# Transformer block with a conditioned norm: the first hundred microseconds in a new order, key rows filled by ScalarE, modulation mostly on VectorE

## The chip, the cores and the metric

The kernel runs on one core of a Trainium2 chip. A core has five engines with an instruction stream each: TensorE (PE in the profile; its weight loads are shown apart as PEld), VectorE (DVE), ScalarE (ACT), GpSimd (POOL) and SyncE (SP), which here does nothing but issue transfers. Within a stream instructions go in order, and an instruction that waits holds up all behind it. The metric is the device time of one execution in microseconds (us); less is better. Two kernels are compared by the medians of several executions.

## The reference

2048 tokens of width 512 pass through attention and a gated feed-forward part; one row `c` of 512 numbers conditions both.

```python
mod = silu(c) @ w_mod                       # six rows of 512: sa, ca, ga, sb, cb, gb
h = layernorm(x) * (1 + ca) + sa            # the first modulation: shift sa, scale 1 + ca
q, k, v = split(h @ wqkv)                   # 32 heads of 16
p = softmax(mask(q @ k.T * 16 ** -0.5))     # key at most 255 behind the query
x = x + ga * ((p @ v) @ wo)                 # gate row ga
h = layernorm(x) * (1 + cb) + sb            # second modulation
x = x + gb * ((silu(h @ w1) * (h @ w3)) @ w2)
```

## The kernel before

Tokens are cut into 4 blocks of 512 (16 tiles of 128), the width into 4 pieces of 128, called k below. Full precision comes from splitting each operand into a high part, rounded to the fast matmul type, and a low rest: one product is three matmuls (high by high, low by high, high by low).

The program has three stages. The **opening** (to about 99 us) loads `x` and the weights, makes the first modulation, normalises all four blocks, transposes them to `hT`, multiplies them by the value weights, and prepares the first three units of attention. A **unit** is one group of 4 heads in one block. The **attention** stage then runs 32 units, and the **feed-forward** stage the rest. In the opening the work on one block goes like this:

- `stats` (L626, L627): mean and variance of a tile on DVE; `root` (L633): the inverse root of the variance on POOL; `apply` (L636): the tile normalised, on DVE.
- `turn` (L641): four PE transposes bring piece k of the block's four tiles into one PSUM bank.
- `shifted` (L645): ScalarE reads that bank, multiplies by 1 + ca and adds sa (columns of `modc`), and writes `h`; `part` (L650, L652): DVE casts `h` to the high part of `hT` and subtracts it to get the low part.
- `value` (L657): three matmuls for a token tile and a piece k, 48 for a block; `value_out` (L661) stores the result to `vS`.
- `product` (L483): a unit's projection for queries and keys, 12 matmuls, evacuated by ScalarE (L489 to L495), mixed by POOL (L501) and written by SP (L506) into `ring`, where queries and keys stand as rows.
- `scores` (L539) and `top` (L546): PE products and DVE maxima which give each query's bound; these rows go into `ring` too (L571).

The first modulation is made on PE: `mod_rows` (L667) multiplies 128 x 128 pieces of `w_mod` by a single column of silu(c), 32 matmuls with one output column each, and `mod_out` (L671) puts sa and 1 + ca into `modc`, one pair of columns per k. The second modulation is made on DVE by `mod_cols` (L675): a row of weights multiplied by `crep` and summed, one column per instruction. `crep` is silu(c) on all 128 partitions; `c` is loaded 128 times for it (L710). The gates ga and gb are rows of PE products (`gate_row`, L682). The value weights' high part is cast by ScalarE (`wvh`, L723) and the low part made by POOL (`wvl`, L725). Constant rows of `ring` beside the keys are set by POOL (`ring_fill`, L453 to L457, five instructions per block). Before all this five products of zeros (L715) occupy PE.

The order in the opening is set by a list scheduler: every step has a key (a planned time) and an assumed duration, engines take what is ready by key, and `OFF0` holds a correction to each step's key, empty here. The scheduler only fixes the order in which instructions stand in each stream; waits are semaphores. All buffers of the opening, `stage` among them (the loads of weights, which lie in the part of `vS` not yet used), are given out in that order. The attention stage has another order, by fixed times within a unit of 8 steps: there `gate_load` (L981) spreads a gate row for `jobs` on POOL (L986) which multiply weights by it.

Of the kernel before, what the change touches and what calls it, by code (L numbers as in the profile page):

```python
# [18 lines left out]
P = 128  # L19
# [24 lines left out]
OFF0 = ()  # L44
K0 = dict(wv=(7.0, 8.5), wl=1.0, h0=11.0, hb=19.0, tn=3.0, st=8.0, ap=4.0, mj=(22.0, 24.0), mg=(24.0, 40.0), rf=(13.0, 23.0, 40.0, 60.0),
# [43 lines left out]
class Op:  # L89
    __slots__ = ("eng", "fn", "occ", "key", "lat", "mode", "deps", "need", "est", "start", "users",  # L90
                 "bank", "seq", "tag", "kb", "base", "more", "port", "att", "quick",
                 "frees")
# [12 lines left out]
class Clock:  # L105
# [5 lines left out]
    def run(self, s, occ):  # L111
# [6 lines left out]
        self.busy += occ  # L118
        return occ


class Sched:
# [7 lines left out]
    def op(self, eng, fn, occ, key, reads=(), writes=(), lat=None, mode=0, port=None):  # L130
# [6 lines left out]
        o.att, o.quick, o.frees = False, False, None  # L137
# [24 lines left out]
    def deal(self):  # L162
# [20 lines left out]
        while left:  # L183
# [63 lines left out]
            if o.eng == "PE":  # L247
                more = clock.run(s, o.occ) - o.occ
                o.occ += more
                o.lat += more  # L250
# [83 lines left out]
def block_kernel(ctx: ExitStack, tc: tile.TileContext, x, wqk, wv, wo, w13, w2, c, crow, wmod, wmodt, out):  # L334
# [270 lines left out]
    XS = 6  # L605
    begin = []

    def do(t, eng, fn, reads=(), writes=(), occ=0.5, kb=0, port=None):
        begin.append((t, len(begin), eng, fn, list(reads), list(writes), occ, kb, port))
# [19 lines left out]
    def var(b):  # L629
        nc.vector.tensor_scalar_add(rs[:, b, 0], mv[:, 4 * b:4 * b + 4, 1], EPS)  # L630

    def root(b):
        nc.gpsimd.tensor_tensor(out=rs[:, b, 1], in0=rs[:, b, 0], in1=nhalf, op=ALU.pow)  # L633

    def apply(t):
        nc.vector.tensor_scalar(xt[t], xt[t], mv[:, t, 0:1], rs[:, t // 4, 1, t % 4:t % 4 + 1],  # L636
                                op0=ALU.subtract, op1=ALU.mult)
# [9 lines left out]
    def part(b, k, n):  # L647
        lo = slice(b * BT, b * BT + BT)
        if n == 0:
# [5 lines left out]
    def value(t, k, bk):  # L655
        for m, (w, i) in enumerate(((0, wvh), (0, wvl), (1, wvh))):
# [17 lines left out]
    def mod_cols(j, n, i):  # L674
        nc.vector.tensor_tensor_reduce(out=stage[:, i], in0=stage[:, i], in1=crep, scale=1.0, scalar=0.0,  # L675
                                       op0=ALU.mult, op1=ALU.add, accum_out=modc[:, 2 + j, n:n + 1])
        if j and n == KC - 1:
# [20 lines left out]
    for t in range(4):  # L698
        dma(0.1 + 0.1 * t, load_x(t), [("xt", t)], eng="ACT" if t in (1, 3) else "SP")
    do(0.6, "ACT", lambda: nc.scalar.activation(sc, c_sb, AF.Silu), ["c"], ["sc"], 1.4)  # L700
    n0 = 0.7
    for n in range(KC):
        for j in range(2):
            dma(n0, lambda j=j, n=n: nc.sync.dma_start(stage[:, KC + KC * j + n], wmod[j, n].rearrange(
                "p k c -> p (k c)")), [("stg", KC + KC * j + n)])
            n0 += 0.1
        dma(n0, lambda n=n: nc.sync.dma_start(stage[:, n], wv[:, n]), [("stg", n)])
        n0 += 0.1
    dma(n0, lambda: load_wqk(0, 0), ["wqr"])
    dma(n0 + 0.1, lambda: nc.sync.dma_start(crep, crow.to_broadcast([P, D])), ["crep"])  # L710
    for t in range(4, 6):
        dma(n0 + 0.2, load_x(t), [("xt", t)])
    for n in range(5):
        bk = Bank("at")
        do(0.5 + 0.1 * n, "PE", lambda bk=bk: nc.tensor.matmul(ps(bk)[:4], zero[:, 0], zero[:, 0, 0:1].to_broadcast([P, BT]),  # L715
# [1019 lines left out]
```

## Time and profile before

| | |
|---|---|
| median of 3 runs (range) | 959.72 us (957.61 to 960.27) |
| the profiled execution, its own time | 957.99 us |
| its span, first to last instruction | 956.3 us |
| mean granted TensorE clock | 0.990 |
| PE busy | 940.2 us, 98% of the span |
| DVE, ACT, POOL busy | 738.7, 549.4, 521.6 us |
| first projection product (L483) | starts at 20.95 us |
| first score product of the attention stage (L857) | starts at 98.91 us |

PE is called busy for nearly the whole span, so the busy share says little. What tells is which matmuls fill the time, how long one takes at a given place, and when each stage begins. Rows of the time line have start, duration, engine, line, operation, output and inputs, count, and in brackets the idle time before with what ended it.

### The profile page before, as it was taken

To read this page: it belongs to the slowest core of one execution; us is meant where nothing else is said; L and a number is where in the kernel's file an instruction comes from. 1 tells how busy PE (TensorE), PEld (TensorE's weight loads), DVE (VectorE), ACT (ScalarE), POOL (GpSimd) and SP (SyncE) were. 2 spreads that over 40 slices of the span, in tenths; PEclk is the share of its full clock that TensorE was granted. 3 is DMA by queue.
4 is the path that set the end of the run, shared out by engine and by line. 5 is a ranking of instruction groups with operands and counts; after the bars stand their busy time and mean duration, and the time that the engine had idled before them with its cause. 6 is when DMAs were issued, how large, how long until landed. Compare 5 with 4: busy or idle time off the path is not lost.

```text
span 956.3 us, 17149 instructions
## 1 busy us (share of the span) xinstructions
PE 940.2 (98%) x5322; PEld 724.5 (76%) x5322; DVE 738.7 (77%) x2055; ACT 549.4 (57%) x1247; POOL 521.6 (55%) x737
## 2 busy tenths in 40 slices
PE   9999999999999999999999999999999999999998
PEld 6667777777777776775688888888888888888886
DVE  6976789998989898989578775676579866677555
ACT  3333787878787878786769854424455334433230
POOL 8611686878686868685643855445767222221320
PEclk7999999999999999999999999999999999999999
DMA  9611354444454444445993564656685422322002
GB/s 327 199 58 36 103 169 153 146 152 143 147 178 139 151 145 146 137 132 178 254 263 121 180 204 135 196 165 210 216 278 172 167 63 79 99 73 87 23 23 88
DMA packets 81702, 141.90 MB, mean 148 GB/s; under 512 B 10570, under 2 KB 23242, under 8 KB 81612
## 3 DMA queue, kind: packets, MB, share of 16 engines
q1 hardware_dynamic: 81180, 140.29, 45.5%
q8 instruction: 42, 0.69, 0.3%
q10 hardware_dynamic: 432, 0.53, 0.2%
q14 instruction: 48, 0.39, 0.1%
HBM read 85.99 MB, written 34.61 MB: 126 GB/s over the span
## 4 chain that ended last, share of the span: by engine, by line
PE 83%; POOL 5%; DMA 4%; DVE 3%; issue 2%; ACT 2%; SPq 0%; POOLq 0%; ACTq 0%; DVEq 0%
PE st L1505 12%; PE mx L1505 10%; PE pj L483 7%; PE mx L539 7%; PE st L857 7%; PE mx L1599 7%; PE po L818 6%; PE st L1599 5%; PE pj L1505 3%; PE mx L657 3%; PE po L1505 3%; PE po L1599 2%; PE pj L1599 2%; POOL pt L885 2%; POOL qk L501 2%
## 5 line engine op out<-in xcount | busy, mean ns | idle before, releaser
L546 DVE CUSTOM_DVE_ANT_0 junk<-mx,mskq 128x384 bf16<-128x384 f32 (+1 forms) x483 | 242.1, 527 | 30.7 <-PE mx L539 29.2
L539 PE MATMUL mx<-ring 96*128 96x384 f32 (+1 forms) x483 | 145.1, 341 | 3.5 <-DVE st L875 1.7
L857 PE MATMUL st<-ring 100*128 100x384 f32 (+2 forms) x484 | 145.9, 343 | 0.6 <-ACT pt L878 0.4
L885 POOL TENSOR_SCALAR_AFFINE_SELECT pt<-pt 128x256 f32<-128x256 f32 x268 | 108.3, 407 | 58.7 <-ACT pt L878 48.4
L483 PE MATMUL pj<-hT,wq 128*128 128x512 f32 x384 | 134.3, 408 | 0.0
L539 PEld LDWEIGHTS mx<-ring 96*128 96x128 f32 x483 | 88.0, 189 | 34.3 <-DVE mt L546 21.7
L878 ACT ACTIVATE pt<-st 128x256 f32<-128x256 f32 x255 | 91.4, 387 | 37.6 <-DVE st L875 30.3
L857 PEld LDWEIGHTS st<-ring 100*128 100x128 f32 x484 | 90.3, 190 | 18.2 <-issue 6.7
L1549 POOL TENSOR_TENSOR t<-t,t 128x512 f32<-128x512 f32 x28 | 40.9, 1460 | 110.9 <-DVE t L1537 103.9
L818 PE MATMUL po<-pt,vS 128*17 128x256 f32 (+2 forms) x1408 | 96.4, 387 | 2.9 <-ACT os L925 1.1
L501 POOL TENSOR_TENSOR qk<-qkr,qk 128x512 fp32r<-128x512 f32 x64 | 83.4, 1303 | 16.5 <-ACT qkr L489 16.3
L1096 POOL TENSOR_TENSOR w<-w,w 128x512 fp32r<-128x512 f32 (+2 forms) x35 | 51.6, 1485 | 57.4 <-ACT w L1095 57.4
L483 PEld LDWEIGHTS pj<-hT,wq 128*128 128x128 f32 x384 | 72.0, 192 | 7.2 <-DVE hT L652 0.2
L1537 DVE TENSOR_TENSOR t<-st,t 128x512 f32<-128x512 f32 x55 | 37.8, 690 | 49.4 <-PE st L1505 37.7
L875 DVE COPY_PREDICATED st<-later,st 128x128 f32<-128x128 uint8 x255 | 68.7, 291 | 7.0 <-PE st L857 3.7
L818 PEld LDWEIGHTS po<-pt,vS 128*17 128x17 f32 x1408 | 32.5, 96 | 47.8 <-issue 18.8
L1505 PE MATMUL st<-b,w 128*128 128x512 f32 x234 | 58.8, 389 | 0.0
L902 POOL TENSOR_SCALAR_AFFINE_SELECT sm<-sm 128x256 f32<-128x256 f32 x109 | 41.9, 407 | 27.1 <-ACT sm L892 23.2
L869 ACT ACTIVATE pt<-st 128x384 f32<-128x384 f32 (+2 forms) x113 | 47.1, 433 | 13.7 <-DVE st L865 12.6
L1505 PE MATMUL mx<-b,w 128*128 128x512 f32 x204 | 51.4, 390 | 0.0
L1505 PEld LDWEIGHTS st<-b,w 128*128 128x128 f32 x234 | 43.9, 188 | 9.2
L1577 ACT ACTIVATE qkr<-g 128x512 fp32r<-128x512 f32 x13 | 8.2, 632 | 66.4 <-DVE g L1533 66.4
(345 smaller groups left out, 2168.4 us busy)
## 6 DMA issues: line engine op xcount, KB each, us to landing
ring<-qk SPq DMA_DIRECT2D x192, 128.0 KB
o_dr<-os SPq DMA_DIRECT2D x32, 256.0 KB
w<-wsum SPq DMA_DIRECT2D x14, 512.0 KB
w<-w2g SPq DMA_DIRECT2D x14, 512.0 KB
jb<-in_w SPq DMA_DIRECT2D x24, 256.0 KB
wraw<-in_w SPq DMA_DIRECT2D x7, 768.0 KB
w<-wraw SPq DMA_DIRECT2D x14, 384.0 KB
e<-in_w SPq DMA_DIRECT2D x18, 256.0 KB
```

The source lines that it names most:

```text
L483: nc.tensor.matmul(v["ps"], WQ[g][w][:, n // 3], hTp(i, n // 3, b * BT, BT), start=(n == 0), stop=(n == 3 * KC - 1))
L501: nc.gpsimd.tensor_tensor(out=v[n], in0=v["raw"], in1=v[1].bitcast(F32), op=ALU.subtract)
L539: nc.tensor.matmul(v[i][:, :n], queries(NS, a, gq, 1), keys(NS, hh, a, k0, gq + 1 - k0), start=True, stop=True)
L546: nc.vector.tensor_tensor_reduce(out=junk[:, :n], in0=v[i][:, :n], in1=mskq[:, 3 * P - n:], scale=1.0, scalar=-3e38, op0=ALU.add, op1=ALU. ...
L818: nc.tensor.matmul(po[32 * i:32 * i + DH + 1, qb * P:(qb + nq) * P], vS[:, kb, 4 * g + i], pts[i // 2][:, i % 2, c0:c0 + nq], start=first, ...
L857: nc.tensor.matmul(ps[:, :nq], keys(NM, hh, a, kb, 1), queries(NM, a, kb, nq), start=True, stop=not plus)
L875: nc.vector.copy_predicated(ps[:, 0], later, ps[:, 2])
L878: nc.scalar.activation(pt_of(j, a)[:, hh, :2], v[j, a, hh][:, :2], AF.Exp, scale=SCALE)
L885: nc.gpsimd.affine_select(out=pt[:, :, 2 * m], in_=pt[:, :, 0], **w)
L1096: sch.op(eng, lambda: on_eng(eng).tensor_tensor(out=lo(), in0=src(), in1=hi().bitcast(F32), op=ALU.subtract), tt(eng, n), key, kl + kh, kl ...
L1505: nc.tensor.matmul(ps(bk), WT[s, n][w][:, col], BB[t, k][r], start=start and c == 0, stop=stop and c == 5, skip_group_check=True)
L1599: nc.tensor.matmul(ps(bk), tiles[hk + (h,)][:, i * P:(i + 1) * P], w2_of(last, y, f), start=(m == 0), stop=(m == 5))
```

## The change

The opening gets other steps and another order; the attention stage changes in one key. The parts:

- **Key rows on ScalarE.** `ring_fill` is two ScalarE copies per block of 100 x 2 x 512 elements, from a small constant tile `fills`, in place of five POOL memsets.
- **First modulation.** Only k = 0 stays on PE (8 of 32 matmuls). For k = 1, 2, 3 `mod_cols` makes the columns on DVE (six instructions and three that add 1), from weights that are loaded the other way round.
- **The condition.** `c` is loaded once as a row, and one PE product with a column of ones spreads it to 128 partitions in PSUM; ScalarE's silu writes `crep` from there. The load of 128 copies is gone.
- **Block 0 normalised in pieces.** The inverse root is taken for two tiles at a time; `apply` is a scalar_tensor_tensor on DVE, first for the 128 columns of k = 0 and then for the other 384.
- **High parts on ScalarE.** In blocks 0 and 1 the high part of `hT` is written by ScalarE from PSUM, beside `shifted`; DVE's cast is gone there.
- **Value weights.** `wvl` for k = 0 is on DVE. In block 0 `value` is cut in two steps: the two products that need only the high part of `hT`, and the third.
- **Idle products.** Five of 512 columns go around the row product; ten of 128 columns follow `mod_rows`.
- **Transfers.** Tile 3 of `x` is issued by SP and not by ScalarE's queue.
- **Order.** Other keys, durations and a table `OFF0`.
- **Attention.** `gate_load` moves from 8u + 7.65 to 8u + 7.85, behind the rows of `ring` that were behind it.

On ScalarE the work before and after the first two `shifted` stands like this; before:

```order
L700 ACTIVATE sc<-c_sb 128x4 [waits DMAHW0_49]
L723 ACTIVATE wvh<-vS 128x512 [waits DMAHW7_49]
L723 ACTIVATE wvh<-vS 128x512 [waits DMAHW2_49]
L723 ACTIVATE wvh<-vS 128x512 [waits DMAHW5_49]
L645 ACTIVATE h_246<-st,modc 128x512 [waits PE_49]
L723 ACTIVATE wvh<-vS 128x512 [waits DMAHW0_49]
L468 ACTIVATE wq_261<-wqr 128x512 [waits DMAHW1_49]
L645 ACTIVATE h_266<-mx,modc 128x512 [waits DVE_49,PE_49]
```

and ScalarE now (L491 is `ring_fill`, L842 the silu that writes `crep`, L780 `wvh`, L687 `shifted`, L692 the high part):

```order
L748 ACTIVATE sc<-c_sb 128x4 [waits DMAHW0_49]
L491 ACTIVATE ring<-fills 100x2x512 [waits Pool_49]
L842 ACTIVATE crep<-st 128x512 [waits PE_49]
L491 ACTIVATE ring<-fills 100x2x512 [waits Pool_49]
L780 ACTIVATE wvh<-vS 128x512 [waits DMAHW0_49]
L780 ACTIVATE wvh<-vS 128x512 [waits DMAHW3_49]
L491 ACTIVATE ring<-fills 100x2x512 x2
L780 ACTIVATE wvh<-vS 128x512 [waits DMAHW6_49]
L687 ACTIVATE h_254<-st,modc 128x512 [waits PE_49]
L692 ACTIVATE hT<-st,modc 128x512
```

(Rows that only repeat are left out: each of the first three fills shown is followed by a second one or has one more beside a `wvh`, so that two fills stand ahead of L842, two between it and the first `wvh`, one between the first and second `wvh`, and two ahead of the third.) Seven of the eight fills stand ahead of the first `shifted`.

On DVE the stretch from the inverse roots to the first low part of `hT`; before:

```order
L630 TENSOR_SCALAR rs<-mv 128x4 [waits DVE_49]
L636 TENSOR_SCALAR xt_130<-xt_130,mv,rs 128x512 [waits Pool_49]
L671 TENSOR_TENSOR modc<-mx,plus 128x2 [waits PE_49]
L636 TENSOR_SCALAR xt_135<-xt_135,mv,rs 128x512
L636 TENSOR_SCALAR xt_137<-xt_137,mv,rs 128x512
L636 TENSOR_SCALAR xt_145<-xt_145,mv,rs 128x512
L671 TENSOR_TENSOR modc<-st,plus 128x2 [waits PE_49] x2
L650 CAST hT<-h_246 128x512 [waits Activation_49]
L652 TENSOR_TENSOR hT<-h_246,hT 128x512 [waits DVE_49]
```

and DVE now (L674 `apply`, L783 `wvl`, L721 `mod_cols`, L697 the low part):

```order
L783 TENSOR_TENSOR wvl<-vS,wvh 128x512 [waits DMAHW0_49,Activation_49]
L674 SCALAR_TENSOR_TENSOR xt_137<-xt_137,mv,rs 128x128 [waits Pool_49]
L674 SCALAR_TENSOR_TENSOR xt_137<-xt_137,mv,rs 128x384
L717 TENSOR_TENSOR modc<-st,plus 128x2 [waits PE_49]
L721 ISA vS,modc<-vS,crep 128x512 [waits DMAHW1_49]
L674 SCALAR_TENSOR_TENSOR xt_143<-xt_143,mv,rs 128x128
L674 SCALAR_TENSOR_TENSOR xt_143<-xt_143,mv,rs 128x384
L674 SCALAR_TENSOR_TENSOR xt_141<-xt_141,mv,rs 128x384
L721 ISA vS,modc<-vS,crep 128x512 [waits DMAHW7_49]
L721 ISA vS,modc<-vS,crep 128x512 [waits DMAHW2_49,DMAHW0_49]
L721 ISA vS,modc<-vS,crep 128x512 [waits DMAHW2_49]
L697 TENSOR_TENSOR hT<-h_254,hT 128x512 [waits Activation_49]
```

(Left out: behind each L721 row the reading of its sum, and behind the last two of them an addition of 1, L724.) `wvl` and four modulation columns now stand between the pieces of `apply` and the first low part. On PE what stands before the first value products; before it was 32 `mod_rows` with transposes between them and then projections, and now:

```order
L764 MATMUL po<-zero 4x512 x3
L757 MATMUL st<-vS,plus 128x512 [waits DMAHW2_49,Pool_49]
L764 MATMUL po<-zero 4x512
L713 MATMUL st<-sc,vS 128x1 [waits DMAHW6_49,Activation_49]
L713 MATMUL st<-sc,vS 128x1 [waits DMAHW7_49]
L764 MATMUL po<-zero 4x128 x10
L683 MATMUL st<-ident,xt_133 128x128 [waits DMAHW1_49,DVE_49,Pool_49]
L703 MATMUL st<-wvh,hT 128x512 [waits Activation_49]
L703 MATMUL st<-wvl,hT 128x512
L703 MATMUL st<-wvh,hT 128x512 [waits DVE_49]
```

(Each L713 row has three more behind it, and 16 transposes L683 stand in a row.) From the first score product of the attention stage on, PE, DVE, ScalarE and POOL have the same instructions in the same order as before. On SP the gate's load; before:

```order
L506 DMA ring<-qk_1568 16x4x512 x2
L506 DMA ring<-qk_1536 16x4x512 x2
L981 DMA wqr<-g_dr 128x512
L506 DMA ring<-qk_1576 16x4x512 x2
L1000 DMA wsum<-jb_1399 128x512
```

and now:

```order
L541 DMA ring<-qk_1553 16x4x512 x2
L541 DMA ring<-qk_1521 16x4x512 x2
L541 DMA ring<-qk_1561 16x4x512 x2
L1055 DMA wqr<-g_dr 128x512
L1074 DMA wsum<-jb_1384 128x512
```

One pair of rows has passed it, at six places. The diff, without the table of offsets and without the scheduler's bookkeeping:

```diff
-OFF0 = ()
+OFF0 = (0, 0, 0, 0, 0, 0, -58.96, -114.58, 0, 0, 0, -188.94, 0, 0, 0, 0, 0, 0, 0, 0, -95.27, 0, 0, 62.42, 0,
...
-    def ring_fill(b, n):
-        hh = int(n > 1)
-        k = ring.bitcast(F32)[:, 2 - 2 * hh, :, b * BT:(b + 1) * BT]
-        if n in (0, 2):
-            nc.gpsimd.memset(k[:NM] if hh == 0 else k[:NS], 0.0)
-        elif n == 3:
-            nc.gpsimd.memset(k[NS:NM], 1.0)
-        else:
-            nc.gpsimd.memset(k[NS:NS + 2], 1.0 - hh)
+    def ring_fill(b, hh):
+        nc.scalar.activation(ring[:NM, 2 - 2 * hh, :, b * BT:(b + 1) * BT],
+                             fills[:NM, hh:hh + 1, None].to_broadcast([NM, 2, BT]), AF.Copy)
...
-            (nc.scalar if t in (1, 3) else nc.sync).dma_start(xt[t], x[t * P:(t + 1) * P, :])
+            (nc.scalar if t == 1 else nc.sync).dma_start(xt[t], x[t * P:(t + 1) * P, :])
...
-    def apply(t):
-        nc.vector.tensor_scalar(xt[t], xt[t], mv[:, t, 0:1], rs[:, t // 4, 1, t % 4:t % 4 + 1],
-                                op0=ALU.subtract, op1=ALU.mult)
+    def apply(t, c):
+        m, r, z = mv[:, t, 0:1], rs[:, t // 4, 1, t % 4:t % 4 + 1], xt[t][:, slice(c * P, D if c else P)]
+        if t < 4 and (t, c) not in K0["ag"]:
+            nc.vector.scalar_tensor_tensor(out=z, in0=z, scalar=m, in1=r.to_broadcast([P, D - P if c else P]),
+                                           op0=ALU.subtract, op1=ALU.mult)
+            return
...
-    def part(b, k, n):
+    def part(b, k, n, bk=None):
         lo = slice(b * BT, b * BT + BT)
-        if n == 0:
+        if n == 0 and b in CAST:
+            nc.scalar.activation(hT[:, 0, k, lo], ps(bk), AF.Identity, bias=modc[:, 0, k:k + 1],
+                                 scale=modc[:, 1, k:k + 1])
+        elif n == 0:
             nc.vector.tensor_copy(hT[:, 0, k, lo], hs[b, k])
...
+    loads = [(KC + KC * j + n, wmod[j, n].rearrange("p k c -> p (k c)")) for n in range(1) for j in range(2)]
+    loads += [(KC + KC * j + n, wmodt[4 * KC + 2 * n + j - 2]) for n in range(1, KC) for j in range(2)]
...
+    dma(0.05, lambda: nc.scalar.dma_start(stage[:1, 3 * KC - 1], crow), [("stg", 3 * KC - 1)], kb=4, eng="ACT")
+    ck = Bank("at")
+    do(0.62, "PE", lambda: nc.tensor.matmul(ps(ck), plus[:1, 1:2].to_broadcast([1, P]), stage[:1, 3 * KC - 1], start=True,
+                                            stop=True), [("stg", 3 * KC - 1)], [ck], 0.87)
...
-    dma(n0 + 0.1, lambda: nc.sync.dma_start(crep, crow.to_broadcast([P, D])), ["crep"])
...
+            if n < 1:
+                do(6.0 + 1.4 * n + 0.7 * j, "PE", lambda j=j, n=n, bk=bk: mod_rows(j, n, bk), ["sc", ("stg", i)],
+                   [bk], 0.9, use=0.03)
+            else:
+                do(K0["mc"] + 1.3 * n + 0.6 * j, "DVE", lambda j=j, n=n, i=i: mod_cols(j, n, i), ["crep", ("stg", i)],
+                   [("stg", i), ("mod", n)], 0.80 if j else 0.70, port=True)
...
-    do(13.0, "ACT", lambda: nc.scalar.activation(crep, crep, AF.Silu), ["crep"], ["crep"], 0.48)
+    do(K0["cs"], "ACT", lambda: nc.scalar.activation(crep, ps(ck), AF.Silu), [ck], ["crep"], 0.66)
...
-            at(8 * u + 7.65, lambda u=u: gate_load(int(u > 6)))
+            at(8 * u + 7.85, lambda u=u: gate_load(int(u > 6)))
```

More of the change, by code (lines that the diff above doesn't have):

```diff
@@ L247, in deal @@
             if o.eng == "PE":
-                more = clock.run(s, o.occ) - o.occ
+                more = clock.run(s, o.occ, o.use) - o.occ
                 o.occ += more
@@ L653, in part, with value @@
                                     op=ALU.subtract)
-    def value(t, k, bk):
-        for m, (w, i) in enumerate(((0, wvh), (0, wvl), (1, wvh))):
+    def value(t, k, bk, r=range(3)):
+        for m in r:
+            w, i = ((0, wvh), (0, wvl), (1, wvh))[m]
             nc.tensor.matmul(ps(bk), hTp(w, k, t * P, P), i[:, k], start=(k == 0 and m == 0),
@@ L713, in block_kernel @@
[L713 to L722 removed]
+        loads.insert(3 * n + 2, (n, wv[:, n]))
@@ L734, in block_kernel @@
     do(12.5, "DVE", fill_odd, [], ["odd"], 0.5)
[L735 removed]
+    do(11.0, "POOL", lambda: nc.gpsimd.memset(vS[:, :4, :, DH:], 1.0), [], ["ones"], 0.35)
     for b in range(NB):
         h = K0["h0"] + K0["hb"] * b
[L738 to L739 removed]
+        for n in range(2):
+            do(K0["rf"][b] + 1.0 * n, "ACT", lambda b=b, n=n: ring_fill(b, n), ["sc"], [("fill", b)], 1.03)
         for i in range(4):
```

138 lines of the change are left out of this document (81 added, 57 removed), and 35 rows, old and new, of the table OFF0.

## The prediction

> **What bounds the kernel now.** I read the page's chain first, then the stretches of the three stages, then PE's time line in the opening. The chain that ends last is PE's:
>
> ```profile
> PE 83%; POOL 5%; DMA 4%; DVE 3%; issue 2%; ACT 2%; SPq 0%; POOLq 0%; ACTq 0%; DVEq 0%
> ```
>
> So the change counts only where it lets PE start real work earlier, or leaves PE with fewer gaps. The stretches (busy time of each engine with its count, then granted clock, DMA share, GB/s) say where that can be:
>
> ```profile
> 0.00:41.70 41.70, 40.03 (x158) 27.32 (x158) 33.05 (x63) 12.63 (x20) 34.00 (x45) 0.84 0.81 277
> 41.70:98.90 57.20, 56.42 (x262) 42.70 (x262) 38.91 (x118) 20.61 (x34) 10.06 (x9) 1.00 0.18 57
> 98.90:956.30 857.40, 843.71 (x4904) 654.45 (x4902) 666.73 (x1875) 516.13 (x1194) 477.53 (x684) 1.00 0.46 148
> ...
> 10.00:15.00 5.00, 4.70 (x31) 4.64 (x31) 4.00 (x5) 1.26 (x2) 4.86 (x5) 0.75 1.05 394
> 20.00:25.00 5.00, 5.00 (x18) 4.22 (x19) 3.90 (x7) 1.73 (x3) 4.83 (x7) 0.50 1.06 338
> 25.00:30.00 5.00, 5.00 (x21) 4.02 (x20) 4.90 (x13) 0.97 (x2) 2.39 (x3) 0.88 0.78 277
> ```
>
> The last 857.4 us keep their order on four engines, so what can move is the first 98.9. There the granted clock is lost between 10 and 26 us, POOL is nearly full (34.0 of 41.7), and ScalarE is nearly idle (12.6). PE is called busy all along, but look at what it does:
>
> ```profile
> 1.10 5.01 PE L715 MATMUL st<-zero 128*4 128x512 f32 x6 [1.10 <-POOL zero L343]
> 5.95 1.89 PE L715 MATMUL mx<-zero 128*4 128x512 f32 x4
> 7.76 1.95 PE L667 MATMUL mx<-sc,vS 128*128 128x1 f32 x16
> 12.20 3.24 PE L667 MATMUL st<-sc,vS 128*128 128x1 f32 x16 [0.30 <-DMA vS<-in_wmod]
> ...
> 20.95 1.63 PE L483 MATMUL pj<-hT,wq 128*128 128x512 f32 x3
> 25.79 0.58 PE L657 MATMUL st<-wvh,hT 128*128 128x512 f32 x1
> 26.21 0.39 PE L657 MATMUL st<-wvl,hT 128*128 128x512 f32 x1
> ...
> 32.40 4.89 PE mx L657 x21
> ...
> 37.23 1.02 PE L682 MATMUL mx<-vS,sc 128*1 128x512 f32 x2
> 41.74 1.53 PE L641 MATMUL st<-ident,xt 128*128 128x128 f32 x12
> 65.68 0.45 PE L539 MATMUL st<-ring 96*128 96x384 f32 x1 [0.47 <-DVE mt L546]
> 98.91 0.34 PE L857 MATMUL st<-ring 100*128 100x384 f32 x1
> ```
>
> A value product takes 4.89 / 21 = 0.233 us at full clock. The ones at 25.79 and 26.21 start 0.42 us apart, so the clock was half until about 26. By 26.21 ten value and projection products are done, worth 2.3 us: PE's real work has a virtual start at 26.2 - 2.3 = 23.9 us. From there block 0 has 60 products (14.0 us) and four gate rows of two passes (the two passes at 37.23 spread 1.02 with their drain; eight make about 3.6), and ends at 41.5; the row at 41.74 agrees. Real work is dense from the virtual start on, so the change is worth what it does to that number, and to the gaps behind it.
>
> **The change, part by part.** The prices:
>
> ```profile
> 0.99 0.48 DVE L399 MEMSET po<- 128x512 f32 x1 [0.99 <-PEq L1727]
> 9.06 0.63 ACT L723 ACTIVATE wvh<-vS 128x512 fp32r<-128x512 f32 x1 [5.02 <-DMA vS<-in_wv]
> 17.11 0.62 ACT L723 ACTIVATE wvh<-vS 128x512 fp32r<-128x512 f32 x1
> 17.63 0.62 ACT L468 ACTIVATE wq<-wqr 128x512 fp32r<-128x512 f32 x1
> 42.49 2.12 ACT L645 ACTIVATE h<-st,modc 128x512 f32<-128x512 f32 x3
> ...
> 9.41 0.55 DVE L636 TENSOR_SCALAR xt<-xt,mv,rs 128x512 f32<-128x512 f32 x1 [1.22 <-POOL rs L633]
> 23.45 0.69 DVE L652 TENSOR_TENSOR hT<-h,hT 128x512 fp32r<-128x512 f32 x1
> 28.25 0.69 DVE L626 BATCH_NORM_STATS2 bst<-xt 128x6 f32<-128x512 f32 x1
> 29.07 0.66 DVE L675 CUSTOM_DVE_ANT_0 vS<-vS,crep 128x512 f32<-128x512 f32 x1
> 29.66 0.69 DVE L675 CUSTOM_DVE_ANT_0 vS<-vS,crep 128x512 f32<-128x512 f32 x1
> 31.45 3.08 POOL L501 TENSOR_TENSOR qk<-qkr,qk 128x512 fp32r<-128x512 f32 x2 [3.97 <-ACT qkr L489]
> 33.30 1.77 DVE L675 CUSTOM_DVE_ANT_0 vS<-vS,crep 128x512 f32<-128x512 f32 x1
> ```
>
> *PE until the row product.* The first idle product now waits for the memset of `po` (0.99 + 0.48 = 1.47). Each is two passes: five at half clock (0.85 each, from 5.01 for six overlapping), the sixth across the switch at 5.95, two more at 0.43 (the spacing in the second row, four in 1.89 with the last's drain): 7.2 us. The row product is two such passes: 8.1 us.
>
> *ScalarE.* A 512-element copy follows the last at 0.52 us (17.11 to 17.63). A fill of 1024 elements has no row; its bounds are 0.52 (as one copy) and 1.04 (as two). I take 0.95, near the upper end, since twice the elements at one fixed cost is near two. From 8.1: `crep` 0.5, two fills 1.9, `wvh` 0.5, fill 0.95, `wvh` 0.5, two fills 1.9, `wvh` 0.5 = 14.9 us for the first `shifted`. The loads are there by then: before, `wvh` was last held by its load at 9.06. A `shifted` or high part follows the last at 0.67 (three in 2.12), and the second of the pair ends 0.8 after it starts: the first high part stands at 14.9 + 0.7 + 0.8 = 16.4.
>
> *DVE up to there.* `wvl` waits for `wvh` (end 8.1 + 0.5 + 1.9 + 0.6 = 11.1) and takes 0.69. Then 128 and 384 columns of `apply`, one addition, one modulation column, 128 columns: about 0.2 + 0.5 + 0.15 + 0.6 + 0.2 (pieces of the 0.55 to 0.69 of full rows) = 13.5, or 14.8 if POOL's `wvl` holds the port; the four transposes follow in 0.5. That is 14.0 to 15.3 against ScalarE's 14.9, so I add 0.3: PE starts value products at 16.7, where the first projection was at 20.95.
>
> *DVE behind it.* Two pieces of 384 columns, three modulation columns at 0.6 (29.07 to 29.66), two additions, the low part 0.65: 13.5 + 3.7 = 17.2 without any blocking. But the row at 33.30 shows a modulation column of 1.77 us where POOL was mixing (31.45 to 34.5), against 0.66 at 29.07: 1.1 more. Now `wvl` for k = 1 and 2 on POOL falls beside these columns. I take one blocking in full: 18.3. PE by then has done four products and waits for the low part. The next thing PE waits for on DVE is the low part of the last k. Ahead of it on DVE stand three tiles' statistics (0.8 each, 28.25 to 29.07), a weight's low part and three of `hT` (2.6), four columns (2.4) and an addition (0.1): 7.6 us, and 1.1 for a third `wvl`: 27.0. PE then has 33 products (7.7) and a gate row (0.9) behind it, so its virtual start is 27.0 - 8.6 = 18.4. The bounds: 17.4 if PE waits only for the first low part (18.3 less four products, 0.9), and 20.6 if two more of these steps lose 1.1.
>
> The Trainium skill, "SBUF — State Buffer", section "Who interferes with whom", speaks against the change here: a VectorE instruction with two SBUF inputs contends with a GpSimd instruction that reads SBUF, and the second to issue fully blocks; modulation columns, low parts and the new form of `apply` all have two such inputs. By that rule every overlap with `wvl` costs its rest, and the virtual start would lie at the upper bound; the row at 33.30 agrees with the rule, that at 29.07 ran with POOL silent.
>
> *The clock.* It fell around 12.2 (the products of one column went from 0.12 to 0.20 us apart) and came back at 26, after a stretch in which PE had full products only. Ten idle products of 128 columns (about 2.1 us) and the missing 24 `mod_rows` are to hold it. Between 13 and 16.7 PE has only transposes, at most 2 us; it may fall there. If half clock lasts from 16.2 to 23, PE has done 0.9 + (23 - 18.3) / 2 = 3.3 us by 23, a virtual start of 19.7; if it holds, 18.4. I take 19.1, between the two: **a gain of 23.9 - 19.1 = 4.8 us**.
>
> *POOL's fills.* 20 memsets of some 1.04 us leave POOL. Their cover was that only `root` and the mixing waited for them. What goes with them is their hold on DVE, which widens the margin below. No time of its own.
>
> *Casts, loads, tile 3.* The cast of two blocks leaves DVE (8 instructions) for ScalarE, which was idle three quarters of the opening: in the sum above. The loads run at a DMA share of 1.05 in the stretch at 10 us; the load of 128 copies of `c` is gone but stood behind all that PE waits for, and tile 3's later issue changes no byte ahead of the weights: nothing.
>
> *Block 1.* PE ends block 0, with four gate rows, at 19.1 + 14.0 + 3.6 = 36.7. Behind 27.0 DVE has a column 0.6, statistics of three more tiles 2.5 with `root` beside them, and four `apply` at 0.55: 5.4 us, so 32.4. A margin of 4.3 us hides it.
>
> *The end of the opening.* The rows there:
>
> ```profile
> 98.86 0.81 SPq L999 DMA_DIRECT2D jb<-in_w  x2
> 101.70 2.08 POOL L995 TENSOR_TENSOR jb<-jb 128x128 f32<-128x128 f32 x4 [22.23 <-DMA jb<-in_w]
> 104.67 0.84 PE L818 MATMUL po<-pt,vS 128*17 128x384 f32 x8 [0.61 <-POOL pt L885]
> ```
>
> The last value product frees the job's tile; load, POOL's job and its masks then hold PE 0.61 us. Now three projections stand between that product and the first score product, where one stood: 0.47 us more cover, **0.4 us gained**. Scores and values also interleave otherwise from 42 to 99: there 54.8 us of products fill 57.2, gaps like that at 65.68 make 2.4. They may shrink or grow by 2; I take no change.
>
> *The gate's load.*
>
> ```profile
> 370.87 1.34 SPq L981 DMA_DIRECT2D wqr<-g_dr  x1
> 375.94 0.41 PE L539 MATMUL mx<-ring 96*128 96x384 f32 x1 [0.71 <-DMA ring<-qk]
> ...
> 327.29 1.27 POOL L986 TENSOR_TENSOR jb<-jb,wqr 128x512 f32<-128x512 f32 x1 [0.69 <-DMA wqr<-g_dr]
> ```
>
> Rows that go first can save PE the 0.71 us at 375.94; the gate comes about 1.2 us later, which adds to POOL's 0.69 at 327.29. Bounds -0.7 and +1.2, four of six places show neither: zero.
>
> **Sum.** 4.8 + 0.4 = 5.2 us off the profiled execution's 957.99 (span 956.3): **952.8 us**. That execution lies 1.7 below the median of 959.72, inside the runs' own range. About 0.3% (2.9 us) is what a measurement of this kernel can tell from no change.
>
> **Rivals.** *The clock stays down* until 26.4 or the low parts come at the upper bound: 0.9 + (26.4 - 18.3) / 2 = 5.0 us done by 26.4, a virtual start of 21.4, and with one more blocking of DVE 22: a gain of 1.9 + 0.4, **955.7**, inside 0.3%. For it speaks that transposes alone fill 13 to 16.7; against it that value products at half clock keep PE full, which brought the clock back before. The Trainium skill, "TensorE: Matmul & The Clock Gate", Part 1, has the clock go back to full after one busy window of about 3.4 us; by that rule dense products from 18.3 on end the half clock by 23 at the latest, and the trace agrees with it as far as the return at 26 goes.
>
> *VectorE becomes the bound* (slower). It was at 4.90 of 5 us already in the stretch from 25, and gets six columns, three additions and a `wvl`. Five blockings more than I count (by POOL's `wvl`, a weight's low part and two mixes before block 1, 1.2 each) make 6 us, and the next tiles, whose loads wait in SP's line behind columns that DVE must read, come some 4 us later: `apply` of block 1 ends at 42.4, 0.7 us after the turn's old place. Blocks 2 and 3 inherit about 1.2 each: 3 us slower, **961**. It decides where DVE is more than 4.3 + 5.2 = 9.5 us later than my count. Against it: 20 memsets no longer hold DVE, and eight casts are gone.
>
> *The new interleaving closes the gaps*: up to 2.4 us more, and the virtual start at 17.4: 948.7. It is the low end of my forecast.
>
> **Chances.** Forecast with its low end 0.62 (faster), the clock or blocking 0.23 (same), DVE the bound 0.15 (slower). The range 948.7 to 959.5 leaves a tenth above, within the slow rival, and little below; the forecast's own is 948.7 to 955.
>
> **What would show it.** The first value product (L703) at 16.7 and the first low part (L697) at 18.3; fills (L491) of 0.95 to 1.05; modulation columns (L721) of 0.66 with some near 1.8; the granted clock above 0.5 before 23; block 1's transposes (L683) at 37; the first L931 near 94; from there 857 us as before. Wrong it goes if L703 starts after 20, if the clock stays half past 26, or if PE waits for DVE at block 1's transposes.

## The result: 0.16% faster, a third of the forecast

| | before | after |
|---|---|---|
| median of ten executions, us | 957.85 (955.89 to 960.27) | 956.26 (955.05 to 957.73) |
| ratio, with its 95% interval | | 0.9984 (0.9972 to 0.9996) |
| profiled execution, us (span) | 957.99 (956.3) | 956.27 (954.6) |

The forecast was 952.8 us. The time fell, but by 1.6 us and not by 5.2. The chain of waits is PE's, more than before:

```profile
PE 86%; POOL 4%; DVE 3%; DMA 3%; ACT 2%; issue 1%; SPq 1%; POOLq 0%; ACTq 0%; DVEq 0%
```

The stretches of the kernel after, cut where block 1's transposes and the attention stage's first score product begin, then the five microseconds that were at half clock:

```profile
0.00:35.70 35.70, 30.47 (x125) 16.24 (x125) 30.82 (x69) 21.91 (x31) 14.23 (x30) 1.00 0.85 295
35.70:92.90 57.20, 56.79 (x269) 44.15 (x269) 40.00 (x122) 22.80 (x38) 8.22 (x8) 1.00 0.22 70
92.90:954.50 861.60, 850.00 (x4904) 654.55 (x4902) 663.48 (x1875) 516.37 (x1195) 476.45 (x684) 1.00 0.46 148
...
20.00:25.00 5.00, 5.00 (x19) 2.85 (x18) 4.93 (x11) 2.71 (x5) 1.27 (x1) 1.00 1.01 341
```

The opening is 6 us shorter (92.9 for 98.9) and the clock is full in it. But the last stretch, which was to stay at 857.4 us, has become 861.6 us with the same 4904 PE records in it. PE's time line in the opening:

```profile
6.55 1.12 PE L757 MATMUL st<-vS,plus 1*128 1x512 f32 x2
10.44 2.38 PE L764 MATMUL po<-zero 128*4 128x128 f32 x20
16.47 0.47 PE L703 MATMUL st<-wvh,hT 128*128 128x512 f32 x1
19.17 0.73 PE L703 MATMUL st<-wvh,hT 128*128 128x512 f32 x2 [1.54 <-DVE hT L697]
29.13 0.50 PE L703 MATMUL st<-wvh,hT 128*128 128x512 f32 x1 [0.51 <-DVE hT L697]
35.72 0.67 PE L683 MATMUL mx<-ident,xt 128*128 128x128 f32 x4
92.94 0.34 PE L931 MATMUL st<-ring 100*128 100x384 f32 x1
98.11 1.06 PE L892 MATMUL po<-pt,vS 128*17 128x384 f32 x8
```

Value products start at 16.47, block 1's transposes at 35.72 (41.74 before), the first L931 at 92.94 (98.91 before), and the products of `po` at 98.11 no longer wait. So where do the 6 us go? Three marks tell: the first attention output that ScalarE takes out of PSUM, the first product of the feed-forward stage, and the last ones. The time lines of the kernel before:

```profile
112.96 0.60 ACT L925 ACTIVATE os<-po 128x512 f32<-128x512 f32 x1 [0.69 <-PE po L818]
521.48 1.54 PE L1505 MATMUL st<-b,w 128*128 128x512 f32 x6
946.20 2.91 PE L1599 MATMUL st<-w,wq 128*128 128x512 f32 x12
948.95 2.91 PE L1599 MATMUL mx<-w,wq 128*128 128x512 f32 x12
```

and of the kernel after:

```profile
106.63 0.60 ACT L999 ACTIVATE os<-po 128x512 f32<-128x512 f32 x1 [0.70 <-PE po L892]
513.58 1.55 PE L1579 MATMUL st<-b,w 128*128 128x512 f32 x6
944.57 2.96 PE L1673 MATMUL st<-w,wq 128*128 128x512 f32 x12
947.37 2.96 PE L1673 MATMUL mx<-w,wq 128*128 128x512 f32 x12
```

The lead is 6.3 us at the first output, 7.9 at the first feed-forward product, and 1.6 at the last ones. The attention stage won 1.6 us more. The feed-forward stage, whose products the diff does not touch and in which PE hardly idles, takes 433.8 + 2.96 = 436.75 us (from 513.58 to the end of the last row) where it took 430.38. The last rows show how: twelve products of one kind take 2.75 us from start to start before (948.95 - 946.20, 229 ns each), and 2.80 us after (233 ns each), at a granted clock of 1.00 in both.

### The profile page after: what moved, and what is told of

The parts are those of the page before. It is cut to its first block, busy times and chain, and to the rows that moved or that the text cites. A ratio compares the mean times of both kernels' runs of the same rounds, so it can differ in the third digit from the quotient of the medians.

```text
span 954.6 us, 17091 instructions
## 1 busy us (share of the span) xinstructions
PE 937.3 (98%) x5296; PEld 714.9 (75%) x5296; DVE 734.3 (77%) x2065; ACT 561.1 (59%) x1263; POOL 498.9 (52%) x721
## 4 chain that ended last, share of the span: by engine, by line
PE 86%; POOL 4%; DVE 3%; DMA 3%; ACT 2%; issue 1%; SPq 1%; POOLq 0%; ACTq 0%; DVEq 0%
PE st L1579 12%; PE mx L1579 10%; PE pj L518 8%; PE mx L574 7%; PE st L931 7%; PE mx L1673 7%; PE po L892 7%; PE st L1673 5%; PE pj L1579 3%; PE po L1579 3%; PE mx L703 2%; PE po L1673 2%; PE st L1315 2%; PE pj L1673 2%; PE mx L1315 2%; PE st L703 2%
## 5 line engine op out<-in xcount | busy, mean ns | idle before, releaser
L931 PE MATMUL st<-ring 100*128 100x384 f32 (+2 forms) x484 | 146.2, 343 | 1.0 <-ACT pt L952 0.4
L574 PE MATMUL mx<-ring 96*128 96x384 f32 (+2 forms) x482 | 144.6, 340 | 1.7 <-ACT pt L943 0.6
L518 PE MATMUL pj<-hT,wq 128*128 128x512 f32 x384 | 132.1, 403 | 0.0
L931 PEld LDWEIGHTS st<-ring 100*128 100x128 f32 x484 | 90.2, 189 | 18.8 <-issue 6.7
L943 ACT ACTIVATE pt<-st 128x384 f32<-128x384 f32 (+2 forms) x113 | 47.1, 433 | 14.9 <-DVE st L939 13.7
```

The costliest lines, as they stand in the source:

```text
L518: nc.tensor.matmul(v["ps"], WQ[g][w][:, n // 3], hTp(i, n // 3, b * BT, BT), start=(n == 0), stop=(n == 3 * KC - 1))
L574: nc.tensor.matmul(v[i][:, :n], queries(NS, a, gq, 1), keys(NS, hh, a, k0, gq + 1 - k0), start=True, stop=True)
L931: nc.tensor.matmul(ps[:, :nq], keys(NM, hh, a, kb, 1), queries(NM, a, kb, nq), start=True, stop=not plus)
```

## The experiments

Where a spacing of products in ns is given below, it is the mean distance from the start of one product to the start of the next in the trace's feed-forward stage, over those that follow each other directly.

### The eight bytes of `fills`

`fills` is a new tile of eight bytes. The built programs tell where tiles lie in a partition of SBUF. The new tile took up 32, and every tile that is allocated behind it on the left side lies 32 bytes higher than before; the right side did not move:

```
                        before    after
vS    (left)             17312    17344
b000  (left, streamed)   17312    17344
w20   (left, streamed)  103328   103360
wo0   (right, weights)  158304   158304
wq00  (right, weights)  211552   211552
```

1240 of the 1848 feed-forward products stream an operand from the left and hold weights from the right; 608 have both on the left. My theory P: the places set the rate. Its rival R: the rate belongs to the execution, or to how hard the core was driven in the opening. The first four runs move nothing but tiles. Old places, in the new kernel:

```diff
-    plus = cst.tile([P, 2], F32, name="plus")
+    plus = cst.tile([P, 4], F32, name="plus")
...
-    fills = cst.tile([P, 2], F32, name="fills")
+    fills = plus[:, 2:4]
```

> The changed kernel, with the eight bytes of `fills` kept in unused bytes of the tile `plus` and not in a tile of their own. Everything allocated on the left side of SBUF then lies 32 bytes lower, at the addresses that it has in the kernel before; the order of the instructions is that of the changed kernel. Theory P (places): a 128x512 product of the feed-forward stage takes as long as the places of its two operands let it; the 32 bytes made those that read one operand from the left side and one from the right slower by about 4.5 ns (229.3 to 233.8 ns from one to the next), and some 1,100 of them gave back about 5 us of the 8 that the opening and the attention had gained. It expects 229.3 ns for these products again and 956.3 - 5.5 = about 950.5 us, 0.992 to 0.993 of the kernel before. Theory R (run): the rate of the matmuls belongs to the execution, the chip or to how hard the core was driven in the opening, not to places. It expects 233.8 ns as in the changed kernel and 956.3 us.

Measured: 948.74 us (947.72 to 951.81), 0.9909 of the kernel before (0.9893 to 0.9925). Its time line:

```profile
106.71 0.60 ACT L999 ACTIVATE os<-po 128x512 f32<-128x512 f32 x1 [0.69 <-PE po L892]
511.46 1.54 PE L1579 MATMUL st<-b,w 128*128 128x512 f32 x6
936.13 2.91 PE L1673 MATMUL st<-w,wq 128*128 128x512 f32 x12
938.88 2.92 PE L1673 MATMUL mx<-w,wq 128*128 128x512 f32 x12
```

The feed-forward stage is back at 430.3 us, twelve products at 2.75. Eight bytes put elsewhere are worth 7.5 us of this kernel, and with the old places the change is 0.9% faster, more than was forecast for it. R has fallen. The reverse, in the kernel before:

```diff
     mskk = mskr.bitcast(F32)
+    cst.tile([P, 2], F32, name="fills")
```

> The kernel before with nothing added but an unused tile of eight bytes where the changed kernel has `fills`: all left-side tiles lie 32 bytes higher, no instruction differs. Theory P expects products of the feed-forward stage with operands from both sides at 233.8 ns, and so 957.9 + 5.5 = about 963 us less what the places give to the attention stage (up to 2 us), 961 to 963.5. Theory R expects 957.9 us and 229.3 ns.

Measured: 964.73 us, 1.0071 of the kernel before (1.0056 to 1.0085); 233.9 ns for the products of `w` with `wq` where they had 229.3. An unused tile, no instruction changed, 0.7% slower. Then the left side another 32 bytes up:

```diff
+    cst.tile([P, 2], F32, name="spare")
     fills = cst.tile([P, 2], F32, name="fills")
```

> The changed kernel with one more unused tile of eight bytes: the left side lies 64 bytes higher than in the kernel before. Theory P in the form that the remainder of the addresses by 64 counts expects the time of the kernel with the old places, about 950.5 us, and 229.3 ns a product. Theory P in the form that the whole address counts leaves it open, between 950 and 958. Theory R expects 956.3 us.

Measured: 955.07 us (0.9970, 0.9960 to 0.9981), products from both sides at 232.5 ns. So it is not the remainder by 64 of the left side. And the right side 32 bytes down:

```diff
+    a1.tile([P, 2], F32, name="spare")
     hx = ExitStack()
```

> The changed kernel with an unused tile of eight bytes on the right side: hT and the feed-forward tiles on the right lie 32 bytes lower, so that they have the remainder by 64 of the left ones again (0 and 0, where the kernel before has 32 and 32, the changed one 0 and 32). Theory P, if what counts is whether both operands have the same remainder: about 950.5 us and 229 ns a product. If what counts is that an operand lies at remainder 0: slower than the changed kernel, about 961 us, with products of two right-side operands (226.7 ns now) slower too. Theory R expects 956.3 us.

Measured: 955.96 us (0.9981, 0.9973 to 0.9990), no gain over the kernel after; 233.3 ns on average for the moved and for the unmoved weights. An equal remainder by 64 does not help either. (Placed there, the spare tile moved `hT`, `wo`, `o` and `x1` but not `wq` and `qk`, which I had missed in the expectation; the same holds of the next run.) What fits these layouts best is the distance of the streamed operand from the weights, in remainder by 256: 64 in the kernel before, 96 after, 128 where one side was moved once more. It does not fit the last one exactly: its 588 products with moved weights lie at 128, and average 233.3 ns where the run with the left side 64 up has 232.4 for the same products. Part of that is where moved and unmoved weights take turns (62 products, 237 ns); the moved ones among themselves have 233.0. Three runs were chosen to test the distance. First, distance 0:

```diff
+    a1.tile([P, 48], F32, name="spare")
     hx = ExitStack()
```

> The kernel with the old places on the left side (948.7 us) and an unused tile of 192 bytes on the right: hT and the right-side feed-forward tiles lie 192 bytes lower. What decides the rate, by the five layouts seen so far, is how far the streamed operand of a product lies from the weights of the next one, in remainder by 256: 0 gave 226.9 to 228.1 ns from one product to the next, 64 gave 229.0, 128 gave 232.5 to 233.0, 96 gave 233.5. Here this distance becomes 0 for the products with operands from both sides. Theory P by remainders of 256 expects 227 ns for them in place of 229.3, a feed-forward stage of 430.3 - 1,150 x 2.3 ns = about 427.7 us, and 946 us in all. If the remainder by 64 alone counts, nothing changes here: 948.7 us. If whole addresses count, any value from 427 to 437 us for the stage.

Measured: the products of `b` with `wo` and `o`, whose weights did move, fell from 228.9 to 226.7 ns; those of `w` with `wq` and `qk`, whose weights did not, stayed at 229.0. The stage took 429.0 us, half of what was expected, because half of the products were moved. The time was 949.77 us, no better than 948.74 (both ranges overlap). Then all of the right side, by a spare tile behind all others:

```diff
+            a1.tile([P, 48], F32, name="spare")
             for n, name in enumerate(("wo", "o")):
```

> The kernel with the old places on the left (948.7 us) and an unused tile of 192 bytes at the far end of the right side, so that all of the right side lies 192 bytes lower, the tiles wq and qk too, which stayed in their place in the last layout. Theory P by remainders of 256 expects about 227 ns for the products of w with wq and qk (229.4 and 228.9 now) as for those of b with wo and o (226.7 to 226.8 in the last layout), a feed-forward stage of 430.3 - 2 x 1.3 = about 427.7 us, and 946 us. If these four groups do not follow the remainder, 948 to 949 us.

```profile
514.87 1.52 PE L1580 MATMUL st<-b,w 128*128 128x512 f32 x6
936.78 2.88 PE L1674 MATMUL st<-w,wq 128*128 128x512 f32 x12
939.50 2.88 PE L1674 MATMUL mx<-w,wq 128*128 128x512 f32 x12
```

Measured: every group at 226.7 ns (2.72 us for twelve), the stage 427.5 us as forecast, and 947.70 us (946.07 to 948.34), 0.9893 of the kernel before (0.9877 to 0.9909), the fastest of all. The kernel gained 1.0 us over the old places and not 2.8: in the profiled execution the feed-forward stage starts 3.4 us later (514.87 for 511.46). Of these, 1.0 us is there at the first attention output (107.67 for 106.71): the granted clock between 15 and 20 us is 0.71 in this execution and 1.00 with the old places. The other 2.4 us arise in the attention stage; it is about as long in the kernel after (406.95 us from that output to the first feed-forward product, 407.20 here), in which `hT` was not moved, so the place of `hT` need not be the cause. It stays open. The two of the four executions with the fuller clock (0.998 on average) took 946.07 and 947.14 us, near the 946 that was expected. Last, the same with 64 bytes (`[P, 16]`), where the theory forecasts a loss:

> The same with 64 bytes in place of 192: the distance of left and right becomes 128 in remainder by 256, with no tile of the left side moved. Theory P by remainders of 256 expects 232.5 to 233 ns for the products with operands from both sides, a feed-forward stage of about 435 us and a time of about 953 us. If what slowed them in the changed kernel is the left side's own place, 229.3 ns and 948.7 us.

```profile
941.70 2.94 PE L1674 MATMUL st<-w,wq 128*128 128x512 f32 x12
944.48 2.96 PE L1674 MATMUL mx<-w,wq 128*128 128x512 f32 x12
```

Measured: 232.5 ns (2.78 us for twelve), a stage of 435.2 us, and 953.41 us in the one execution, all as forecast, with no tile of the left side moved. Together:

| layout | left, right (by 256) | distance | left streamed, right weights (1240), ns | both left (608), ns | stage, us |
|---|---|---|---|---|---|
| before; old places | 160, 96 | 64 | 228.9 | 226.9 | 430.4; 430.3 |
| after; before moved | 192, 96 | 96 | 233.3 | 228.6 | 436.75; 436.8 |
| left 64 up | 224, 96 | 128 | 232.5 | 227.5 | 435.1 |
| right 64 down | 160, 32 | 128 | 232.5 | 227.5 | 435.2 |
| right 192 down | 160, 160 | 0 | 226.7 | 226.7 | 427.5 |

The sum agrees: 1240 x 4.4 + 608 x 1.7 ns = 6.5 us, and the stage lost 6.4. What the last column but one says is less clear: with both operands on the left the distance is always 0, and yet 608 products slow down by up to 1.7 ns when one side is moved against the other. The 548 of them that follow one of their own kind do so too (226.9 before, 228.1 after). The whole rule of addresses stays open; that of the 1240 was forecast twice, and came.

### The gate's load

The forecast had it at zero. In the kernel with the old places it was put back ahead of the ring rows:

```diff
-            at(8 * u + 7.85, lambda u=u: gate_load(int(u > 6)))
+            at(8 * u + 7.65, lambda u=u: gate_load(int(u > 6)))
```

> The kernel with the old places, and the load of the gate's row put back ahead of the ring rows on SP's queue (7.65 for 7.85); PE, DVE, ACT and POOL have the same order. Theory G (the load's place makes the gain inside the attention stage): the lead over the kernel before, which grows from 6.3 us at the first output to 9.3 at the thirtieth, stays at 6.3 to 7, and the time is 948.7 + 2.5 = about 951 us. Theory H (the load is hidden, as was forecast, and the gain there comes from what the opening leaves in the queues, or from places): 948.7 us, and the lead grows as it did.

Measured: 955.94 us (953.34 to 958.79), 7.2 us slower. The groups of PE's score products between 110 and 480 us, with their idle time and what ended it; first this kernel:

```profile
L574 PE MATMUL mx<-ring 96*128 96x384 f32 x391 | 120.8, 350 | 5.1 <-DMA ring<-qk 2.9 <-ACT pt L943 1.5 <-ACT pt L952 0.4
```

the same with the load behind the rows:

```profile
L574 PE MATMUL mx<-ring 96*128 96x384 f32 x391 | 120.5, 349 | 1.1 <-DVE st L949 0.5 <-ACT pt L952 0.4
```

the kernel before:

```profile
L539 PE MATMUL mx<-ring 96*128 96x384 f32 x401 | 124.1, 350 | 3.5 <-DVE st L875 1.7 <-DMA ring<-qk 1.1 <-ACT pt L878 0.4
```

Waits for these ring rows, 2.9 and 1.1 us, are in the kernels with the load ahead; with the load behind no run has more than 0.3. Theory G holds, at more than its price: the direct wait is 2.9 us, the lead lost up to the first feed-forward product 5.6 (517.05 against 511.46) in the profiled execution, which is the fastest of twelve. The rest of the 7.2 I can only argue: rows that come late push the unit behind them. Then the one line in the kernel before:

> The kernel before with only the load of the gate's row put behind the ring rows on SP's queue (7.85 for 7.65). Theory G2 (the load in its old place makes score products wait for ring rows that stand behind it): the wait of PE's scores for DMAs into the ring, 1.7 us between 110 and 480 us, goes, and with it some 2 us: 955 to 956 us. Where the dearer 7 us that the same step cost in the kernel with the old places hold here too, 951 us. Theory H2 (the load is hidden as long as the opening is the old one): 957.6 us.

```profile
L539 PE MATMUL mx<-ring 96*128 96x384 f32 x398 | 122.8, 349 | 2.1 <-ACT pt L869 1.1 <-DVE mr L556 0.7 <-ACT pt L878 0.3
```

Measured: 954.64 us against 958.42 of the kernel before, 0.9965 (0.9955 to 0.9975): 3.8 us from one line, and the wait is gone. With the old places throughout, this gives four corners:

| | load ahead of the rows | load behind |
|---|---|---|
| old opening | 957.6 to 958.4 | 954.6 |
| new opening | 955.9 | 948.7 |

The new opening is worth 1.7 us by itself and 5.9 with the load moved (5.4 by the two ratios to the kernel before, as the runs were on different chips). Why the earlier start makes the load dearer (7.2 for 3.8) was not tried.

### The idle products and the clock

```diff
-        do(t, "PE", lambda n=n: idle_turn(n), [], [], 0.0017 * n, est=t)
+        do(t, "PE", lambda n=n: idle_turn(1 if n == 128 else n), [], [], 0.0017 * n, est=t)
```

> The kernel with the old places, with the ten idle products of 128 columns ahead of the first transposes cut to one column each, in the same place. Theory C (the idle products hold the clock): the clock in the profile falls to a half for a window of 13.7 us or so after 10 us, as in the kernel before; by the forecast this costs 19.7 - 18.4 = 1.3 us of the opening, and as some 3 to 6 us of products would run at half speed at most 3: 950 to 952 us. Theory D (the clock holds without them, since the real products come soon enough): 948.7 us and a clock of 1.00 throughout.

```profile
10.00:15.00 5.00, 2.61 (x30) 1.59 (x29) 4.32 (x10) 4.85 (x8) 2.15 (x2) 0.62 1.04 395
15.00:20.00 5.00, 4.57 (x19) 3.86 (x20) 4.90 (x13) 3.36 (x6) 1.32 (x1) 0.69 1.05 372
```

Those are its stretches of five microseconds (the clock is the third number from the end); its time line:

```profile
17.50 0.73 PE L703 MATMUL st<-wvh,hT 128*128 128x512 f32 x1
19.12 0.73 PE L703 MATMUL st<-wvh,hT 128*128 128x512 f32 x2 [0.19 <-DVE hT L697]
...
106.34 0.60 ACT L999 ACTIVATE os<-po 128x512 f32<-128x512 f32 x1 [0.69 <-PE po L892]
```

Measured: 949.30 us (947.23 to 950.01), where with them it was 948.74 (947.72 to 951.81): no difference that can be told. The clock does fall (0.62 and 0.69 between 10 and 20 us): the first value product comes at 17.50, 0.6 us later than with them (16.91 with the old places). But the fifth product had waited 1.5 us for DVE's low part, and now waits 0.19. The half clock lies in a wait that is there anyway, and the first output comes no later (106.34 for 106.71). Theory C is wrong on the price. That the idle products hold the clock is less sure than this one pair of traces says: in the profiled executions of five other layouts (the left side 64 up, and the four of the new opening that move the right side) the clock fell to between 0.66 and 0.72 from 15 to 20 us with the ten products in place.

### The table of offsets

```diff
-OFF0 = (0, 0, 0, 0, 0, 0, -58.96, -114.58, 0, 0, 0, -188.94, 0, 0, 0, 0, 0, 0, 0, 0, -95.27, 0, 0, 62.42, 0,
...
+OFF0 = ()
```

> The kernel with the old places, with the table of 444 offsets (OFF0) taken out, so that the opening stands in the order that the keys alone give. If the new order is what the opening's gain rests on, the first score product comes some us later and the time is 953 to 957 us; if the parts do it (ScalarE's fills, the row product, VectorE's reductions, the idle products), 949 to 950 us.

```profile
111.07 0.60 ACT L964 ACTIVATE os<-po 128x512 f32<-128x512 f32 x1 [0.69 <-PE po L857]
```

Measured: 953.23 us (951.83 to 953.87), 0.9949 (0.9934 to 0.9963). The time line has the first output at 111.07: of the opening's 6.3 us the order of the table is 4.4, and the parts in the order of their keys 1.9.

### Two lines alone

The kernel before with the load behind the rows and the right side 192 bytes lower:

> The kernel before with two lines alone: the load of the gate's row behind the ring rows (954.6 us by itself) and the right side 192 bytes lower. If the places act by themselves, the feed-forward stage is 427.5 us again, as in the kernel with the same places and the new opening, and the time is 954.6 - 2.9 = 951.8 us. If the places are worth their 2.9 us only behind the new opening, 954.6 us.

Measured: 950.50 us (948.86 to 954.52), 0.9921 (0.9902 to 0.9939), with a feed-forward stage of 427.5 us. The places act by themselves, and two lines give 7.9 us, nearly five times what the whole change gave.

## Why the prediction was half right

*The opening: right, nearly to the step.* The row product ended at 7.7 (forecast 8.1), the first value product stood at 16.47 (16.7), block 1's transposes at 35.72 (36.7), the first L931 at 92.94 (near 94). ScalarE and DVE after:

```profile
3.90 1.99 ACT L491 ACTIVATE ring<-fills 100x1024 fp32r<-100x1024 f32 x2
10.62 1.04 ACT L491 ACTIVATE ring<-fills 100x1024 fp32r<-100x1024 f32 x1
14.60 0.78 ACT L687 ACTIVATE h<-st,modc 128x512 f32<-128x512 f32 x1
...
12.83 2.41 DVE L674 SCALAR_TENSOR_TENSOR xt<-xt,mv,rs 128x128 f32<-128x128 f32 x3
15.16 1.76 DVE L721 CUSTOM_DVE_ANT_0 vS<-vS,crep 128x512 f32<-128x512 f32 x1
18.44 0.68 DVE L697 TENSOR_TENSOR hT<-h,hT 128x512 fp32r<-128x512 f32 x1
26.66 2.41 DVE L697 TENSOR_TENSOR hT<-h,hT 128x512 fp32r<-128x512 f32 x2
32.23 3.78 DVE L679 TENSOR_SCALAR xt<-xt,mv,rs 128x512 f32<-128x512 f32 x4
```

A second fill starts 0.95 us after the first (1.99 - 1.04), the value taken. `shifted` came at 14.60 (14.9). The first low part ended at 19.12, 0.8 us after the 18.3 counted: the sum had one blocking, the modulation column at 15.16 (1.76), and there were two, since three pieces of `apply` took 2.41 us at 12.83, beside an earlier `wvl` on POOL. The column ran beside POOL's next `wvl`; the rule of the Trainium skill that stood in the prediction ("SBUF — State Buffer", section "Who interferes with whom") agrees.

*The last low part and block 1: forecast too early by 2 to 4 us, and it cost little.* The last low part ended at 29.07 and not at 27.0, since the pair at 26.66 lost a blocking too. PE waited 0.51 us there: the scheduler had put gate rows and projections ahead. DVE's `apply` for block 1 starts at 32.23, about when it was forecast to be done (32.4), and ends at 36.01; the margin of 4.3 us was used up, and the transposes at 35.72 still show no wait. The slow rival, DVE as the bound, came nearer than its 0.15 says.

*The clock: right, in part by luck, and worth nothing that could be told.* It held, 1.00 up to block 1's transposes; in five other layouts with the same idle products it did not. The 19.1, taken between 18.4 and 19.7, was too careful: 35.72 - 14.0 - 3.6 is 18.1, and the run without idle products shows that even the half clock would not have cost its 1.3 us.

*The end of the opening and the gaps: right.* The 0.61 us wait for POOL's masks is gone, and from block 1's transposes to the first L931 it is 57.2 us before and after.

*The gate's load at zero: wrong.* It was priced by single waits of 0.71 and 0.69 us, with bounds from -0.7 to +1.2. Moving it is worth 3.8 us in the kernel before, and 7.2 behind the new opening. The 0.71 us row was one instance of six; the same wait stood in the groups of score products as 1.1 us, and each one also delays what follows.

*"From there 857 us as before": the step that failed.* The order of the instructions was the same on four engines, and I took that for the same time. The sum had no term for where the new tile lies, and so put at nothing what cost 6.4 us in the feed-forward stage. The attention stage gained 1.6 us by the profiled marks, the feed-forward stage lost 6.4, and of 6.3 + 1.6 us the 1.6 that were measured are left. By medians, each step against its own neighbour with the other parts as they stand: -1.7 for the opening, -7.2 for the gate's load, +7.5 for the places (956.26 less 948.74), which is -1.4 of the -1.6 measured. That the time lies close to the 955.7 us of the rival in which the clock stays down is chance: the clock did not stay down.

## What to carry to other kernels

An added tile moves everything that its pool allocates behind it: compare the addresses of the operands in the densest product loop of both programs, and if a stage in which nothing was edited changes its time, look at the distance from product to product there before looking for waits. Try a spare tile of 32 to 192 bytes on one side; it costs a line. A load that is not urgent belongs behind the rows that PE is about to wait for, and one wait in the profile is a poor measure of its price: here the wait was 0.71 us and the price 3.8 and 7.2.

## What the runs showed of the hardware

A 128 x 512 product with full clock and no wait takes 226.7 to 233.3 ns, on average, depending on how far its streamed operand lies from the weights in SBUF, by 256 bytes: 226.7 at distance 0, 228.9 at 64, 233.3 at 96, 232.5 at 128. Other distances were not tried. What collides was not shown; that the weights of the next product are read while this one streams is a guess, and the products with both operands on the left, at distance 0 and yet at 226.7 to 228.6, do not bear it out by themselves. The Trainium skill, "SBUF — State Buffer", section "Who interferes with whom", gives PE two independent read ports and lets it wait on no one. The runs differ: products lose up to 3% with the places of their operands, to PE's own reads or to another engine's, which no run separates, and the measurement decides.

POOL's memsets held some of DVE's instructions and not others. In the kernel before a subtraction with two inputs took its full-speed 0.69 us beside one. A cast took 0.43 us with POOL idle, and 1.27 and 1.26 us (at 22.14 and 24.33) beside memsets that started with it. So the hold that the prediction spoke of was there for the casts, and not for the low parts:

```profile
17.24 0.43 DVE L650 CAST hT<-h 128x512 fp32r<-128x512 f32 x1 [1.60 <-ACT h L645]
20.59 1.17 POOL L457 MEMSET ring<- 2x1024 f32 x1
20.91 0.69 DVE L652 TENSOR_TENSOR hT<-h,hT 128x512 fp32r<-128x512 f32 x1
22.14 1.27 DVE L650 CAST hT<-h 128x512 fp32r<-128x512 f32 x1 [0.55 <-ACT h L645]
22.18 0.95 POOL L453 MEMSET ring<- 100x1024 f32 x1
```
